# A pre-norm transformer block on one core: one ordinary group of gate and up products fewer, vector work placed by the list, two x tiles on another queue

## The chip, the core and the metric

The kernel runs on one core of a Trainium2 chip. The metric is the device time of one execution in microseconds (us). Engines are named as in the profile: PE multiplies matrices (PEld is its weight load), DVE is the vector engine, ACT the scalar engine, POOL is GpSimd, SP the engine that issues most DMAs.

## The reference, cut to what matters

The input is one sequence of 2048 tokens with 448 features, all in float32. H is 16, the window W is 256, the hidden width of the feed-forward is 1792.

```python
def _A_ref(x, wqkv, wo):                       # sliding-window attention
    ...
    scores = jnp.einsum("bhqd,bhkd->bhqk", q, k) * (Dh ** -0.5)
    mask = (idx[:, None] - idx[None, :] >= 0) & (idx[:, None] - idx[None, :] < W)
    p = _softmax(jnp.where(mask[None, None], scores, -1e9), axis=-1)
    ...
def _B_ref(x, w_gate, w_up, w_down):           # gated feed-forward
    g = jnp.einsum("bsd,df->bsf", x, w_gate)
    u = jnp.einsum("bsd,df->bsf", x, w_up)
    return jnp.einsum("bsf,fd->bsd", _gelu(g) * u, w_down)

h = x + _A_ref(_layernorm(x), A_wqkv, A_wo)
h2 = h + _B_ref(_layernorm(h), B_w_gate, B_w_up, B_w_down)
```

## The kernel before, in words

Every float32 operand of a product is split into a high and a low part (`to_hi` on ACT, line 396; `to_lo` on DVE or POOL, line 399), and a product is three matmuls: high by high, high by low, low by high.

**Order.** The program is not written in the order in which it runs. Each step is handed to a list (`op`, `dma`) with an engine, a key, an expected duration and the tiles that it reads and writes. `Lists.run` then walks through the list in its own model of time, takes at each point the candidate that can start first, the smaller key ahead, and so fixes what stands in which row of each engine. On the chip every engine works through its rows in that order and waits where an operand is late. The constants at the head of the file (keys, lags, engine names) only move rows.

**Attention.** Sixteen blocks (four chunks of 512 tokens by four groups of heads) go through projections (line 678), scores (729), maxima (733, DVE), probabilities (802, with exponentials at 806, ACT), products with v (840) and the output product (900, into `hres`). The first x tiles are loaded into `hres` by `load` in `start` (line 525), all by SP's queue.

**Feed-forward.** The 2048 tokens by 1792 columns fall into fourteen groups of 256 columns by 1024 tokens. Each group needs gate, up, and the product with `w_down`. A gate or up product of a group can be made in two ways:

- *Ordinary* (`cslot`, line 1139, and `cfull`, line 1151): four turns (two halves of the tokens, gate and up), each of 7 slots. A slot is 6 matmuls of 512 columns, two at a time on the two halves of the rows of PE's array. A group is 28 slots.
- *By seven products* in place of eight, after Strassen's scheme (`both`, line 1340): 25 slots of the same 6 matmuls for gate and up together. This asks for sums and differences of pieces of x (`tokens_x`, lines 1051, 1054 and 1057) and of the weights (`weight_set` with `sum_`, line 1210, on POOL), and for sums of the results (`copied`, 1346, ACT; `added`, 1350, DVE).

The first `CL` groups are ordinary; some of their slots fill waits late in the attention. The rest are made by seven products. Between the slots of a later group stand the down products of an earlier one (`down_half`, line 1414). Their halves write the same four banks one after the other, and before the second half may write, ACT reads one element of the bank (`seen`, line 1260). `out_add` (1431) adds the finished rows to `hres`.

**Buffers.** Weights of a group by seven products lie in one of three areas, `wbuf`: the tile `w2` (shown as `w`) and two halves of `proj`. Pieces of x for the first 1024 tokens lie in `xo` (`xarea`, `XPLACE`), which is opened after the attention, and for the last 1024 tokens in `xT`.

## Time and profile before

| | |
|---|---|
| runs | 696.53, 698.39, 698.69 us; median 698.39 us |
| profiled execution | 698.2 us, of which the span from the first to the last instruction is 696.5 us |
| granted clock | 0.999 |
| PE, DVE, ACT, POOL busy | 98%, 74%, 59%, 45% of the span |
| instructions of PE (matmuls) | 5544, of them 450 ordinary gate/up, 1650 by seven products, 1320 down |
| share of the 16 DMA engines | 58% (SP's queue) |

Busy time says how much of a stretch an engine had work in flight. Windows cut the span into stretches, waits say which engine ended another's idle time, the chain follows the end of the program back to what released each step, and the timeline lists instructions in order of time.

### The profile page before, as it was taken

What the parts mean: (1) busy time and instruction counts of PE and PEld (TensorE: products, weight loads), DVE (VectorE), ACT (ScalarE), POOL (GpSimd) and SP (SyncE); (2) the same over time, 40 slices, a digit from 0 to 9 for tenths busy, and PEclk for the clock granted to TensorE, in tenths of its full rate; (3) what the DMA queues carried; (4) which work ended last, traced back from release to release, by engine and by line L of the source; (5) the groups of instructions that cost most, each with busy time, mean ns of one, the idle gap of its engine ahead of it and who ended that gap; (6) DMA issues with size and microseconds to landing.
All of it is one profiled execution on the core that took longest, in us unless ns stands there. A gap on an engine that the chain in (4) does not pass through costs nothing. (4 is left out here: it accounts for less than half of the span.)

```text
span 696.5 us, 15373 instructions
## 1 busy us (share of the span) xinstructions
PE 685.1 (98%) x5544; PEld 578.1 (83%) x5544; DVE 513.4 (74%) x1213; ACT 413.9 (59%) x911; POOL 311.1 (45%) x422
## 2 busy tenths in 40 slices
PE   8999999999999999999999999999999999999997
PEld 7888888888888878878878888888888888888886
DVE  7967678987798788838775789776555756866764
ACT  7747576877768667776554565644534545546431
POOL 5612654644456446441452779634303445447000
PEclk9999999999999999999999999999999999999999
DMA  9997967688688697406767775415004744533102
GB/s 315 277 285 216 286 173 202 183 230 244 166 210 247 183 273 207 165 1 178 197 181 158 213 205 170 119 51 171 20 16 131 211 132 132 161 116 88 44 15 105
DMA packets 104691, 116.25 MB, mean 167 GB/s; under 512 B 44632, under 2 KB 82392, under 8 KB 104040
## 3 DMA queue, kind: packets, MB, share of 16 engines
q1 hardware_dynamic: 104472, 115.17, 58.0%
q8 instruction: 43, 0.70, 0.4%
q14 instruction: 32, 0.26, 0.1%
q10 hardware_dynamic: 144, 0.11, 0.0%
HBM read 84.97 MB, written 44.47 MB: 186 GB/s over the span
## 5 line engine op out<-in xcount | busy, mean ns | idle before, releaser
L733 DVE CUSTOM_DVE_ANT_0 mt<-bank,mt 128x384 bf16<-128x384 f32 (+2 forms) x256 | 126.4, 526 | 26.8 <-PE bank L729 24.8
L806 ACT ACTIVATE pp<-bank 128x384 f32<-128x384 f32 (+1 forms) x188 | 90.8, 527 | 18.5 <-PE bank L802 16.3
L678 PE MATMUL bank<-xT 128*128 128x512 f32 x308 | 96.1, 399 | 0.0
L1340 PE MATMUL bank<-xT,proj 64*128 64x512 f32 x735 | 94.7, 389 | 0.2 <-DVE v L1350 0.2
L1340 PEld LDWEIGHTS bank<-xT,proj 64*128 64x128 f32 x735 | 72.1, 184 | 13.4 <-DVE v L1350 0.8
L729 PE MATMUL bank<-rk,rq 84*128 84x384 f32 (+2 forms) x256 | 81.0, 337 | 0.0
L802 PE MATMUL bank<-rq,rk 104*128 104x384 f32 (+2 forms) x352 | 80.6, 302 | 0.0
L821 POOL TENSOR_SCALAR_AFFINE_SELECT pp<-pp 128x512 f32<-128x512 f32 x96 | 60.6, 651 | 40.2 <-ACT pp L806 38.6
L1414 PE MATMUL bank<-proj,gh 64*128 64x448 f32 x624 | 71.5, 362 | 1.2 <-ACT e L1260 1.2
L802 PEld LDWEIGHTS bank<-rq,rk 104*128 104x128 f32 x352 | 59.4, 190 | 9.3 <-ACT pp L806 1.5
L1431 DVE TENSOR_TENSOR hres<-bank,hres 128x448 f32<-128x448 f32 (+1 forms) x113 | 62.8, 611 | 5.6 <-PE bank L1414 5.6
L1414 PEld LDWEIGHTS bank<-proj,gh 64*128 64x128 f32 x624 | 59.2, 184 | 8.0 <-ACT e L1260 1.9
L678 PEld LDWEIGHTS bank<-xT 128*128 128x128 f32 x308 | 55.6, 189 | 6.8 <-DVE proj L399 0.5
L1210 POOL TENSOR_TENSOR xn<-proj 64x128 f32<-64x128 f32 (+2 forms) x36 | 33.3, 928 | 52.5 <-DMA proj<-gu 46.8
L1260 ACT ACTIVATE e<-bank 1x1 f32<-1x1 f32 x139 | 21.7, 156 | 55.9 <-PE bank L1414 41.3
L729 PEld LDWEIGHTS bank<-rk,rq 84*128 84x128 f32 x256 | 47.6, 189 | 7.0 <-DVE mx L733 1.4
L396 ACT ACTIVATE rq<-bank 8x512 fp32r<-8x512 f32 x64 | 37.7, 589 | 22.1 <-PE bank L760 21.0
L399 DVE TENSOR_TENSOR proj<-proj 128x448 fp32r<-128x448 f32 (+2 forms) x42 | 25.8, 630 | 32.0 <-ACT proj L396 27.0
L624 PE MATMUL bank<-proj,xT 128*128 128x448 f32 (+1 forms) x220 | 49.1, 334 | 0.0
L1340 PE MATMUL bank<-xo,proj 64*128 64x512 f32 x366 | 47.7, 389 | 0.1
L1340 PEld LDWEIGHTS bank<-xo,proj 64*128 64x128 f32 x366 | 36.0, 184 | 7.1 <-DVE v L1350 0.8
L1350 DVE TENSOR_TENSOR raw<-bank,raw 128x512 f32<-128x512 f32 x22 | 15.2, 691 | 35.1 <-PE bank L1340 35.0
(193 smaller groups left out, 1474.3 us busy)
## 6 DMA issues: line engine op xcount, KB each, us to landing
rk<-k SPq DMA_DIRECT2D x44, 336.0 KB
rq<-q SPq DMA_DIRECT2D x32, 336.0 KB
gu<-in_gu_dram SPq DMA_DIRECT2D x18, 480.0 KB
proj<-gu SPq DMA_DIRECT2D x24, 288.0 KB
q<-proj SPq DMA_DIRECT2D x12, 448.0 KB
proj<-down SPq DMA_DIRECT2D x22, 224.0 KB
proj<-gu SPq DMA_DIRECT2D x24, 192.0 KB
k<-proj SPq DMA_DIRECT2D x9, 448.0 KB
```

The costliest lines, as they stand in the source:

```text
L396: nc.scalar.activation(dst, src, AF.Copy)
L624: op("pe", mm(224 * n), 0.29 if n == 1 else 0.38, key + a / 16, lambda a=a, h=h, wb=wb, xb=xb: nc.tensor.matmul(bank[b.k][:, 0:224 * n], x ...
L678: op("pe", mm(512) + 0.002, 0.403, key, lambda a=a, h=h, wb=wb, xb=xb: nc.tensor.matmul(bank[b.k], wqk[m][:, h, wb, :], xT[:, xb, cc * 128 ...
L729: nc.tensor.matmul(bank[b.k][:, o:384], rq[u][0:3 * DH, j, i * 128:i * 128 + 128], rk[u][0:3 * DH, j, m0 * 128:(i + 3) * 128], start=True, ...
L733: nc.vector.tensor_tensor_reduce(junk[s % 2][:, o:384], bank[b.k][:, o:384], mask[:, o:384], 1.0, -BIG, OP.add, OP.max, mx[:, i, j:j + 1])
L802: nc.tensor.matmul(bank[b.k][:, n * i:n * i + n], rk[u][0:104, j + i, m * 128:m * 128 + 128], rq[u][0:104, j + i, lo * 128:(hi + 1) * 128] ...
L806: nc.scalar.activation(pp_cols(o, n)[:, j:j + G], bank[b.k][:, 0:G * n].rearrange("p (g t) -> p g t", g=G), AF.Exp, scale=SCALE)
L821: nc.gpsimd.affine_select(a, a, pattern=[[0, 4], [-cm, 128]], compare_op=op_, fill=0.0, base=0, channel_multiplier=cm)
L1210: arith("pool", w, key + 1, lambda e: e.tensor_tensor(xn_m[HALF[side], o:o + w], a(), b(), op=what), rd, [tok])
L1340: nc.tensor.matmul(bank[b.k], w, xarea(u.cp, xl, xs, side)[:, xk], start=p in (1, 2, 5) and not k and not t, stop=t == 2, tile_position=(6 ...
L1414: nc.tensor.matmul(bank[banks[q].k][:, 0:D], h[oh][0]()[HALF[x], q * 128:q * 128 + 128], d[wh][0]()[HALF[x]], start=not ph and not y and n ...
L1431: op("dve", 0.07 + w * 0.463 / D, 0.163 + w * 0.463 / D, key, lambda: nc.vector.tensor_tensor(hres[:, t, c0:c0 + w], bank[b.k][:, c0:c0 + ...
```

## The change

One group less is ordinary (`CL` 3 becomes 2), so that twelve groups instead of eleven are made by seven products. The list may now choose the engine, POOL or DVE, of the sums for x and for the weights and of their low parts, and the engine, ACT or DVE, of the copies of results (`alts`, switched on by `FLEX`). Pieces of x for the first tokens are placed partly in `xT`, so that some of their loads can go before the attention ends. Two of the first four x tiles are issued by ACT's queue. A finer token (`XTB`) lets the list place matmuls of the high part of x ahead of the low part. Some forty numbers of the list are others; two of their lines stand here.

```diff
-MERGE = (1, 1, 1, 0, 1, 1, 1, 1, 0, 1, 1, 1)
+MERGE = (1, 1, 1, 0, 1, 1, 1, 1, 1, 0, 0, 1)
...
-CL = 3
+FLEX = 'xwc'
+CL = 2
...
+            o.fn = lambda: alts[o.eng][2]()
...
-                cand[o.eng].append(o)
+                for e in o.alts or (o.eng,):
+                    cand[e].append(o)
...
+                if o.alts and min(start_of(x, o)[0] + o.alts[x][1] for x in o.alts) < t + o.alts[e][1]:
+                    continue
...
+    def XTB(t, xb):
+
+        return span("xT", t, 1) if xb == 3 else span("xT", t + (xb > 3) / 2, 0.5)
...
-        for t in range(4):
+        op("pool", 0.1, 0.1, -101, lambda: nc.gpsimd.memset(nhalf, -0.5), (), ["nhalf"])
+        for t in range(2):
             load(t, -100 + t)
+        op("act", 1.35, 1.45, -110, lambda: nc.scalar.activation(rcp[0][0:1, 0:1], nhalf[0:1, 0:1], AF.Copy), ["nhalf"], [("rcp", 0)])
+        for t in range(2, 4):
+            op("act", 0.44, 2.3 + 0.3 * (t - 2), -110 + t, lambda t=t: nc.scalar.dma_start(hres[:, t, :], xr[t * 128:(t + 1) * 128, :]),
+               (), [HR(t)])
...
+    wbuf = wbuf if CL > 2 else [wbuf[2], *wbuf[:2]]
...
-    def arith(eng, n, key, fn, r, w, port=True):
-        cost = 0.1 + n * 0.00225 if eng == "pool" else 0.07 + n * 0.00104
-        op(eng, cost, cost + (0.05 if eng == "pool" else 0.1), key, lambda: fn(nc.gpsimd if eng == "pool" else nc.vector),
-           r, w, port=port)
+    def arith(eng, n, key, fn, r, w, port=True, free_choice=False):
+        ways = {"pool": (0.1 + n * 0.00225, 0.15 + n * 0.00225, lambda: fn(nc.gpsimd), port),
+                "dve": (0.07 + n * 0.00104, 0.17 + n * 0.00104, lambda: fn(nc.vector), port)}
+        cost, lat, go, _ = ways[eng]
+        op(eng, cost, lat, key, go, r, w, port=port, alts=ways if free_choice else None)
...
-            arith("pool", w, key + 1, lambda e: e.tensor_tensor(xn_m[HALF[side], o:o + w], a(), b(), op=what), rd, [tok])
+            arith("pool", w, key + 1, lambda e: e.tensor_tensor(xn_m[HALF[side], o:o + w], a(), b(), op=what), rd, [tok], free_choice="w" in FLEX)
```

In the built programs PE's matmuls go from 5194 to 5168: 168 fewer of `cslot`, 150 more of `both`, 8 fewer of the transposes of `ident` that only fill time at the start. DVE's instructions go from 1215 to 1346, POOL's from 427 to 328, ACT's stay at 914.

**ACT at the start.** Before, ACT's rows begin with the load of its function table and a fill of `rk` (line 569), and the normalised x tiles (449) follow:

```order
L569 ACT_TABLE_LOAD
L569 ACTIVATE rk_186<-e_75 32x1536
L396 ACTIVATE one<-ident 128x128
L449 ACTIVATE xn<-hres,bnve 128x448 x2
L396 ACTIVATE proj<-pp 128x2x224
```

Now the first row is a DMA of an x tile, and a second one stands behind the table load (lines are numbered as in the changed kernel: 550 issues the tiles, 548 brings the table, 467 normalises):

```order
L550 DMA hres<-in_x_dram 128x448
L548 ACT_TABLE_LOAD
L548 ACTIVATE rcp_81<-bnve 1x1
L550 DMA hres<-in_x_dram 128x448
L414 ACTIVATE one<-ident 128x128
L591 ACTIVATE rk_184<-e_75 32x1536
L467 ACTIVATE xn<-hres,bnve 128x448
```

Two DMA issues have moved from SP to ACT, one of them behind the table load; SP's weight loads stand two issues earlier.

**The first weights by seven products.** Before, the sums of the first weight set (in `w`, line 1210) stand on POOL, with sums for x (1057) between:

```order
L1210 TENSOR_TENSOR xn<-w_3359 128x384
L1057 TENSOR_TENSOR e_3360<-xo,raw 64x512
L399 TENSOR_TENSOR xo<-raw,xo 128x512
L1210 TENSOR_TENSOR xn<-w_3359,xn 128x384
L1210 TENSOR_TENSOR xn<-w_3359 64x128
L1210 TENSOR_TENSOR xn<-w_3359,xn 64x384
L1210 TENSOR_TENSOR xn<-w_3359 64x384
L399 TENSOR_TENSOR w_3359<-xn,w_3359 128x384
L1210 TENSOR_TENSOR xn<-proj 64x128
```

Now the first set lies in `proj`, and its sums (line 1237) stand on DVE, behind the products of gate and up (1206) of an ordinary turn and between the low parts (417) and the sums (1081) of x:

```order
L1206 TENSOR_TENSOR v<-bank_174,v 128x512
L1206 TENSOR_TENSOR v<-bank_175,v 128x512
L417 TENSOR_TENSOR xT<-raw,xo 128x512
L1237 TENSOR_TENSOR xn<-proj 128x384
L1237 TENSOR_TENSOR xn<-proj 64x128
L1237 TENSOR_TENSOR xn<-proj,xn 128x384
L417 TENSOR_TENSOR proj<-proj 128x256
L1237 TENSOR_TENSOR xn<-proj,xn 64x384
L1237 TENSOR_TENSOR xn<-proj 64x384
L417 TENSOR_TENSOR proj<-proj 128x384
L1081 TENSOR_TENSOR raw<-raw,xT 64x512
L417 TENSOR_TENSOR proj<-xn,proj 128x128
```

All five sums of this set have moved to DVE's rows.

More of the change, by code (lines that the diff above doesn't have):

```diff
@@ L1009, in load @@
         def load(l, slot, side, c, row, k0=0, n=1):
-            dma(key, 131 * n, lambda: nc.sync.dma_start(f(xarea(cp, l, slot, side)[:, k0:k0 + n]), rows(c, row + 64 * k0, n)),
+            soon = not cp and type(XPLACE[cp][l, slot]) is tuple
+            dma(X0LOAD + 10 * k0 if soon else key, 131 * n, lambda: nc.sync.dma_start(
+                f(xarea(cp, l, slot, side)[:, k0:k0 + n]), rows(c, row + 64 * k0, n)),
                 come(c) + xgate(cp, l, slot), [t for k in range(k0, k0 + n) for t in xtok(cp, l, slot, k, side)], cost=0.61 + 0.03 * n,
-                after=chain[-1:])
+                after=[got[X0HOLD]] if soon else chain[-1:])
         def fill(k, i, c, row):
```

153 lines of the change are left out of this document (83 added, 70 removed).

## The prediction

> **What bounds the kernel now.** I read the page first, then the span cut into stretches, then the timeline of PE where it waits.
>
> ```profile
> PE 685.1 (98%) x5544; PEld 578.1 (83%) x5544; DVE 513.4 (74%) x1213; ACT 413.9 (59%) x911; POOL 311.1 (45%) x422
> ```
>
> PE is in work for 685.1 of 696.5 us, so the time is PE's stream and its few waits. The stretches are: to the first projection, the attention to its last output product, the ordinary groups, the groups by seven products, the tail. Columns: length, then each engine's busy time and its instructions, granted clock, DMA.
>
> ```profile
> core 0: us, PE busy (x) PEld busy (x) DVE busy (x) ACT busy (x) POOL busy (x), PEclk, DMA share, GB/s
> 0.00:14.07 14.07, 10.63 (x75) 9.87 (x76) 9.66 (x21) 10.20 (x17) 9.61 (x29) 1.00 0.88 299
> 14.07:322.57 308.50, 308.40 (x2168) 253.97 (x2166) 243.88 (x774) 217.82 (x430) 143.21 (x241) 1.00 0.74 209
> 322.57:376.45 53.88, 51.94 (x465) 43.06 (x466) 40.49 (x73) 30.03 (x77) 19.31 (x21) 1.00 0.75 189
> 376.45:673.99 297.54, 296.85 (x2696) 256.35 (x2696) 206.86 (x325) 152.39 (x377) 138.94 (x131) 1.00 0.41 119
> 673.99:696.50 22.51, 17.26 (x147) 14.86 (x145) 12.53 (x23) 3.50 (x13) 0.00 (x0) 0.96 0.23 82
> ```
>
> The attention and the eleven groups by seven products have PE busy but for 0.1 and 0.7 us; the clock is full. One group by seven products takes 297.54 / 11 = 27.05 us. The stretch that waits is the third, 1.94 us. Its timeline on PE (start, length, instructions, in brackets the idle time and who ended it):
>
> ```profile
> 336.99 1.37 PE L1414 MATMUL bank<-proj,gh 64*128 64x448 f32 x12
> 338.85 1.50 PE L1414 MATMUL bank<-proj,gh 64*128 64x448 f32 x12 [0.48 <-ACT e L1260]
> 340.19 2.25 PE L1139 MATMUL bank<-xT,proj 64*128 64x512 f32 x18
> ...
> 345.00 2.61 PE L1414 MATMUL bank<-proj,gh 64*128 64x448 f32 x24
> 347.44 4.95 PE L1139 MATMUL bank<-xT,proj 64*128 64x512 f32 x42
> 352.23 1.37 PE L1414 MATMUL bank<-proj,xT 64*128 64x448 f32 x12
> 354.37 1.50 PE L1414 MATMUL bank<-proj,xT 64*128 64x448 f32 x12 [0.77 <-ACT e L1260]
> 355.71 4.97 PE L1139 MATMUL bank<-xT,proj 64*128 64x512 f32 x42
> 360.51 2.61 PE L1414 MATMUL bank<-proj,e 64*128 64x448 f32 x24
> 362.96 4.95 PE L1139 MATMUL bank<-xT,proj 64*128 64x512 f32 x42
> 367.75 1.37 PE L1414 MATMUL bank<-proj,gh 64*128 64x448 f32 x12
> 369.81 1.48 PE L1414 MATMUL bank<-proj,gh 64*128 64x448 f32 x12 [0.69 <-ACT e L1260]
> 371.13 2.88 PE L1139 MATMUL bank<-xT,proj 64*128 64x512 f32 x24
> 373.85 2.60 PE L1414 MATMUL bank<-proj,gh 64*128 64x448 f32 x24
> 376.28 0.63 PE L1340 MATMUL bank<-xo,w 64*128 64x512 f32 x4
> ```
>
> Two readings. Seven ordinary slots (42 matmuls) go from 347.44 to 352.23, so a slot is 4.80 / 7 = 0.686 us. And 24 down matmuls in one piece take 2.44 us where nothing is late (345.00 to 347.44), but 3.20, 3.48 and 3.38 us (from 336.99, 352.23 and 367.75) where ACT's one-element read of the bank came late: 2.74 us lost in three of six pieces.
>
> **Term 1, the products.** A group leaves the ordinary way, 28 slots, for the other, 25. In the chain of waits a slot by seven products costs the same:
>
> ```profile
> 617.00 2.74 PE bank L1340 x24
> 619.74 1.21 PE bank L1414 x12
> 620.95 2.06 PE bank L1340 x18
> ```
>
> Three slots are 18 matmuls, 2.06 us. All of it lies on PE, which is the path: **-2.06 us**. The built program has these 18 matmuls less, so nothing of this term hangs on a choice of the list.
>
> **Term 2, the pieces of down.** Behind the last output product the new order has 27 ordinary slots instead of 53, and two unbroken pieces of 24 down matmuls instead of six; in all other places halves of down stand between products, where ACT's read has time. At the rate of before, one of two pieces late by 2.74 / 3 = 0.91 us, 0.91 stays of 2.74: **-1.83 us**. Bounds: -2.74 with none late, -0.9 with both.
>
> **Term 3, the cover of the first group by seven products.** Its first product stood 53.88 us behind the attention's last output product, and stands now at 27 x 0.686 + 2 x 2.44 = 23.4 us. Call that output product's end T. The first weight set overwrites what this product reads, so it can only be loaded from T on, and its sums are now DVE's, in a row behind the two products of gate and up of an ordinary turn that PE finishes 16 slots behind T, at T + 11.0. DVE then has 21 instructions to the last low part of these weights: 11 of 512 elements, 7 of 384, three short. Their prices without and with POOL at work beside:
>
> ```profile
> 323.50 1.28 DVE L399 TENSOR_TENSOR gh<-raw,gh 128x512 fp32r<-128x512 f32 x2
> 367.14 0.72 DVE L399 TENSOR_TENSOR w<-xn,w 128x384 fp32r<-128x384 f32 x2
> L1368 DVE TENSOR_TENSOR v<-bank,v 128x512 f32<-128x512 f32 x11 | 7.5, 680 | 0.0
> L1368 DVE TENSOR_TENSOR v<-e,v 128x512 f32<-128x512 f32 x11 | 11.1, 1006 | 0.0
> L399 DVE TENSOR_TENSOR proj<-xn,proj 128x384 fp32r<-128x384 f32 x12 | 7.5, 623 | 0.8 <-ACT proj L396 0.8
> ```
>
> Two of 512 in 1.28 us are 0.64 each or less; 1006 ns is the group that meets POOL's sums most. For 384 elements about 0.47 us (of the 0.72 us for one long and one short), and 623 ns as the mean of its group. With the short ones at 0.3: 11 x 0.64 + 7 x 0.47 + 0.9 = 11.2, ready at T + 22.2 and 1.2 us early; with the dear rows 11 x 1.006 + 7 x 0.623 + 0.9 = 16.3, ready at T + 27.3 and 3.9 us late. Behind these weights stand the last third of the x pieces, which PE wants some 1.4 us after the first slot, so that there is no room. POOL has in these rows only three sums and two chains of small ones, so I stay near the cheap end and take **+0.7 us**; bounds 0 and +5.5 (3.9 with four x instructions more at 0.4 dearer). It cannot gain, because PE did not wait there before.
>
> **Term 4, the start.** Columns of the timeline as above.
>
> ```profile
> 0.79 1.28 ACT L569 ACT_TABLE_LOAD   x1 [0.79 <-PEq L1778]
> 0.79 1.81 SPq L525 DMA_DIRECT2D hres<-in_x_dram  x4
> 3.40 0.63 DVE L428 BATCH_NORM_STATS2 bnst<-hres 128x6 f32<-128x448 f32 x1 [1.42 <-DMA hres<-in_x_dram]
> 5.51 0.63 DVE L428 BATCH_NORM_STATS2 bnst<-hres 128x6 f32<-128x448 f32 x1 [0.54 <-DMA hres<-in_x_dram]
> 7.33 0.23 POOL L419 TENSOR_SCALAR bnve<-bnmv 128x2 f32<-128x2 f32 x1 [0.36 <-DVE bnmv L430]
> 14.07 4.30 PE L678 MATMUL bank<-xT 128*128 128x512 f32 x18
> ```
>
> The third tile goes out at once and DVE's wait of 0.54 us for it can go, but POOL works on the third and fourth as a pair and waited 0.36 us only: no more than that is to be had. The fourth tile's issue moves from 2.1 us (the fourth of four in 1.81) behind the first issue (0.45) and the table load (1.28), to 2.6 us, so as much can be lost; ACT's fill of `rk` behind them has until 5.65 us, when ACT first waits for nothing else. I take **0**, bounds -0.4 and +0.5. [...]
>
> **Term 5, the attention.** The same matmuls in another order, and one block more whose products with v are made in two parts (`MERGE`), which brings one change more of PE's array mode. Its price is the pause of PE's weight load at line 840, 15.4 / 72 = 0.21 us:
>
> ```profile
> PEld bank L840 <- issue: 15.4, 72, 0.4
> PEld bank L1340 <- DVE v L1350: 2.7, 6, 0.8
> ```
>
> **+0.2 us**, bounds 0 and +2 for waits that a new order may open; there are 0.1 us to gain by the stretch's idle time.
>
> **Term 6, the groups by seven products.** DVE's additions kept the weight load waiting six times, 2.7 us (row above). With DVE fuller and POOL emptier this may go either way: 0, bounds -2.7 and upward as in the rival below.
>
> **Sum** on the profiled execution's 698.2 us (its span 696.5 and 1.7 around it): 698.2 - 2.06 - 1.83 + 0.7 + 0.2 = **695.2 us**. The profiled execution lies 0.2 us below the median of the runs, 698.39, so I take the sum as the forecast of the median. 0.3% or 2.1 us is about what can be told from no change here; the forecast is 3.2 us below.
>
> **Rivals.**
> *The cover is gone (0.17).* DVE's chain of term 3 is dear: half way to the bound, 3.5 us late instead of 0.7, gives 698.0 us, no change. For it: the 1006 ns row, and that 53.88 us of cover become 23.4. Against: POOL's few instructions there.
> *DVE becomes the bound (0.15), slower.* In the fourth stretch DVE has 206.86 / 11 = 18.8 us of work in each group's 27.05. The 131 instructions that the list gives it besides are 10.9 in each of twelve groups, if all lie there. The point is (27.05 - 18.8) / 10.9 = 0.76 us apiece: at 0.623 a group has 25.6 us and PE still leads; at 0.85, between the 384 and the 1006 ns row, 28.1 us, so 1.0 us a group and 12.4 in all: 707.6 us. Against it: what dear rows there are come from POOL's work, and POOL has 99 instructions fewer.
> *The port set free (0.08), faster still.* If DVE's dear rows become cheap ones as POOL's sums go, the 2.7 us of waits for its additions go with them: 692.5 us. [...]
> That the change does not do what it says is ruled out for the products, which are counted in the built program.
>
> **Numbers.** The forecast has 0.60, of which I put 0.05 above 696.3 us. Faster by over 0.3%: 0.55 + 0.08 = 0.63. Within: 0.17 + 0.05 = 0.22. Slower: 0.15. The range goes down to 692.0 (the port set free, with a little of the start) and up to 699.5, over the dear chain of term 3 (698.0) and most of its bound (695.2 - 0.7 + 5.5 = 700.0); the DVE-bound case is left out above.
>
> **What would show it.** Right: 282 ordinary matmuls and 1800 by seven products; 27.0 us a group as before; at most one pause of PE with ACT's read at its end before the first product of line 1369, which starts some 23.5 us behind the last output product; at that first group a wait for DVE below 1 us; DVE at 80 to 85% of the fourth stretch. Wrong: a wait of several us for DVE's `proj` or `xT` at the first group (first rival); groups of 28 us with PE waiting for DVE throughout (second); a first projection later than 14.6 us; an attention longer than 308.5 - 1.4 us (two ordinary slots fewer stand in it) by more than 1 us.

## The result and the profile after

The changed kernel takes 709.52 us (median of five runs, 708.89 to 711.16), the kernel before 698.39 us beside it (696.53 to 699.25): a ratio of 1.0173, 95% interval 1.0151 to 1.0196. The forecast of 695.2 us and its range (692.0 to 699.5) missed; the sign was that of the rival to which 0.15 was given. The profiled execution took 709.5 us, its span 707.8. The page's first part, and the span cut at the points of the prediction (first projection, last output product, first product by seven, last one):

```profile
PE 689.3 (97%) x5518; PEld 602.1 (85%) x5518; DVE 561.0 (79%) x1344; ACT 413.8 (58%) x909; POOL 200.7 (28%) x323
0.00:15.61 15.61, 11.03 (x56) 9.99 (x56) 9.17 (x21) 10.39 (x17) 11.04 (x28) 0.78 0.91 319
15.61:324.82 309.21, 308.74 (x2170) 254.44 (x2168) 243.69 (x776) 215.73 (x427) 142.92 (x243) 1.00 0.77 209
324.82:353.10 28.28, 25.19 (x211) 20.74 (x212) 25.95 (x46) 16.98 (x40) 4.67 (x4) 0.94 0.62 142
353.10:684.93 331.83, 327.16 (x2944) 302.22 (x2942) 269.71 (x481) 167.24 (x414) 42.10 (x49) 1.00 0.46 126
684.93:707.80 22.87, 17.23 (x147) 14.76 (x145) 12.53 (x23) 3.50 (x13) 0.00 (x0) 0.93 0.23 81
```

Work has gone from POOL (311.1 to 200.7 us) to DVE (513.4 to 561.0 us), and DVE is now in work for 25.95 of the 28.28 us ahead of the first product. The granted clock is no longer full in two stretches, 8.28 to 15.11 and 346.20 to 349.61 us (0.50 in both). Against the prediction's own sum (T is the end of the last output product):

| | forecast | measured | more |
|---|---|---|---|
| start and attention, to T | 322.57 - 1.37 + 0.2 = 321.4 | 324.8 | 3.4 |
| T to the first product by seven | 23.4 + 0.9 + 0.7 = 25.0 | 28.3 | 3.3 |
| twelve groups | 12 x 27.05 = 324.6 | 331.8 | 7.2 |
| tail | 22.5 | 22.9 | 0.4 |

The groups, of 150 products each, take 29.59, 27.24, 27.23, 30.19, 29.23, 26.87, 26.87, 27.10, 27.01, 27.04, 27.63 and 25.84 us: the excess is in the first, the fourth and the fifth; the eleventh has 0.6 us of it. PE's waits, with who ended them, in us, times, longest:

```profile
PE bank L1445 <- ACT e L1288: 3.1, 1, 3.1
PE bank L472 <- ACT xn L467: 2.4, 2, 1.9
PE bank L1751 <- POOL ident L573: 2.1, 1, 2.1
PE bank L1369 <- DVE xo L417: 1.9, 1, 1.9
PE bank L1369 <- DVE v L1381: 1.3, 2, 1.1
```

The first is one pause in front of the second half of the first down product. PE's timeline shows it and what comes behind it:

```profile
340.53 1.37 PE L1445 MATMUL bank<-proj,gh 64*128 64x448 f32 x12
344.99 1.61 PE L1445 MATMUL bank<-proj,gh 64*128 64x448 f32 x12 [3.09 <-ACT e L1288]
346.40 4.42 PE L1166 MATMUL bank<-xT,w 64*128 64x512 f32 x24
350.65 2.61 PE L1445 MATMUL bank<-proj,gh 64*128 64x448 f32 x24
353.10 0.39 PE L1369 MATMUL bank<-xo,proj 64*128 64x512 f32 x2
```

24 ordinary matmuls take 4.42 us; the 24 ahead of the pause took 2.88. ACT's rows tell why its read (L1288) came late, and some of DVE's rows why ACT was:

```profile
340.59 0.53 ACT L414 ACTIVATE proj<-proj 128x384 fp32r<-128x384 f32 x1 [0.84 <-DMA xn<-v]
341.02 0.75 ACT L467 ACTIVATE raw<-hres,bnve 128x448 f32<-128x448 f32 x1
341.68 0.29 ACT L414 ACTIVATE proj<-xn 128x128 fp32r<-128x128 f32 x1
342.89 0.52 ACT L414 ACTIVATE proj<-xn 128x384 fp32r<-128x384 f32 x1 [0.93 <-DVE xn L1237]
343.32 1.06 ACT L1191 ACTIVATE v<-bank 128x512 f32<-128x512 f32 x2
344.28 0.63 ACT L414 ACTIVATE xo<-raw 128x512 fp32r<-128x512 f32 x1
344.80 0.34 ACT L1288 ACTIVATE e<-bank 1x1 f32<-1x1 f32 x2
...
336.87 1.43 DVE L417 TENSOR_TENSOR xo<-e,xo 128x512 fp32r<-128x512 f32 x1 [1.33 <-ACT xo L414]
338.21 1.28 DVE L1206 TENSOR_TENSOR v<-bank,v 128x512 f32<-128x512 f32 x2
...
340.01 0.86 DVE L1237 TENSOR_TENSOR xn<-proj 128x384 f32<-128x384 f32 x2
...
348.86 0.54 DVE L417 TENSOR_TENSOR proj<-xn,proj 128x384 fp32r<-128x384 f32 x1
```

The read stands behind high parts of the first weights, which wait for transfers (0.84 us ahead of the pause) and for DVE's sums (0.93 us in it); the rest of the pause is ACT's own work in the rows ahead of the read. In the fourth and fifth group it is DVE itself; windows of groups 4 and 5, and DVE's rows where PE waits 1.86 us for the last of them but one:

```profile
437.20:467.30 30.10, 28.50 (x249) 24.05 (x247) 28.85 (x46) 17.90 (x42) 8.78 (x6) 1.00 0.52 146
467.30:496.60 29.30, 27.44 (x251) 26.18 (x249) 23.50 (x40) 12.60 (x32) 3.15 (x4) 1.00 0.36 97
464.94 1.77 DVE L1084 TENSOR_TENSOR v<-xT,v 64x512 f32<-64x512 f32 x1
466.64 1.49 DVE L417 TENSOR_TENSOR e<-v,e 128x512 fp32r<-128x512 f32 x1
468.06 1.48 DVE L417 TENSOR_TENSOR xo<-xo,xT 128x512 fp32r<-128x512 f32 x1
469.47 0.67 DVE L1381 TENSOR_TENSOR raw<-bank,raw 128x512 f32<-128x512 f32 x1
...
463.36 2.81 POOL L417 TENSOR_TENSOR xo<-v,xT 128x512 fp32r<-128x512 f32 x1 [0.42 <-ACT e L1288]
466.25 1.34 POOL L1237 TENSOR_TENSOR xn<-proj 64x384 f32<-64x384 f32 x1
467.67 1.33 POOL L417 TENSOR_TENSOR proj<-proj 128x384 fp32r<-128x384 f32 x1
```

DVE has 28.85 us of work in 30.10, and instructions that take 0.67 us at 344.78 and 346.58 us, with POOL idle, take 1.5 to 1.8 here beside POOL's. Four such rows in group 4 take 3.9 us more than 0.67 each, as much as the group's excess. No run sets DVE free of POOL there and leaves it the same rows, so how much of the loss is the number of rows and how much their price stays open.

### The profile page after: what moved, and what is told of

It is laid out like the page before. It is cut to its first block, busy times and chain, and to the rows that moved or that the text cites. A ratio compares the mean times of both kernels' runs of the same rounds, so it can differ in the third digit from the quotient of the medians.

```text
span 707.8 us, 15249 instructions
## 1 busy us (share of the span) xinstructions
PE 689.3 (97%) x5518; PEld 602.1 (85%) x5518; DVE 561.0 (79%) x1344; ACT 413.8 (58%) x909; POOL 200.7 (28%) x323
## 4 chain that ended last, share of the span: by engine, by line
PE 84%; DVE 10%; DMA 2%; issue 2%; ACT 1%; POOL 0%; SPq 0%; DVEq 0%; ACTq 0%
PE bank L1369 25%; PE bank L1445 16%; PE bank L700 10%; PE bank L824 7%; PE bank L751 6%; PE bank L862 6%; PE bank L646 5%; PE bank L922 4%; PE bank L1178 2%; DVE hres L1462 2%; PE bank L1166 1%; PE bank L472 1%; DVE xo L417 1%; DMA xo<-xn 1%; DVE xT L417 1%
## 5 line engine op out<-in xcount | busy, mean ns | idle before, releaser
L755 DVE CUSTOM_DVE_ANT_0 mt<-bank,mt 128x384 bf16<-128x384 f32 (+2 forms) x256 | 126.8, 525 | 27.8 <-PE bank L751 26.0
L1369 PE MATMUL bank<-xT,proj 64*128 64x512 f32 x627 | 121.6, 388 | 0.0
L1369 PE MATMUL bank<-xo,proj 64*128 64x512 f32 x552 | 111.9, 390 | 3.1 <-DVE xo L417 1.9
L1445 PE MATMUL bank<-proj,gh 64*128 64x448 f32 x672 | 82.2, 365 | 3.8 <-ACT e L1288 3.1
L1369 PEld LDWEIGHTS bank<-xT,proj 64*128 64x128 f32 x627 | 81.2, 184 | 4.4
L1369 PEld LDWEIGHTS bank<-xo,proj 64*128 64x128 f32 x552 | 72.3, 184 | 8.2 <-DVE xo L417 2.3
L1445 PEld LDWEIGHTS bank<-proj,gh 64*128 64x128 f32 x672 | 69.7, 184 | 9.4 <-ACT e L1288 3.5
L1369 PE MATMUL bank<-xT,w 64*128 64x512 f32 x330 | 63.8, 390 | 0.0
L1288 ACT ACTIVATE e<-bank 1x1 f32<-1x1 f32 x132 | 20.7, 157 | 66.9 <-PE bank L1445 51.8
L1369 PE MATMUL bank<-xo,w 64*128 64x512 f32 x255 | 54.0, 389 | 0.4 <-DVE raw L1381 0.4
L646 PE MATMUL bank<-proj,xT 128*128 128x448 f32 (+1 forms) x220 | 51.9, 341 | 0.0
L1369 PEld LDWEIGHTS bank<-xT,w 64*128 64x128 f32 x330 | 43.0, 184 | 3.1 <-DVE v L1381 0.6
```

Of the source, the lines that this page charges most:

```text
L646: op("pe", mm(224 * n), 0.29 if n == 1 else 0.38, key + a / 16, lambda a=a, h=h, wb=wb, xb=xb: nc.tensor.matmul(bank[b.k][:, 0:224 * n], x ...
L755: nc.vector.tensor_tensor_reduce(junk[s % 2][:, o:384], bank[b.k][:, o:384], mask[:, o:384], 1.0, -BIG, OP.add, OP.max, mx[:, i, j:j + 1])
L1369: nc.tensor.matmul(bank[b.k], w, xarea(u.cp, xl, xs, side)[:, xk], start=p in (1, 2, 5) and not k and not t, stop=t == 2, tile_position=(6 ...
L1445: nc.tensor.matmul(bank[banks[q].k][:, 0:D], h[oh][0]()[HALF[x], q * 128:q * 128 + 128], d[wh][0]()[HALF[x]], start=not ph and not y and n ...
```

## The experiments

All runs in one table. First projection, T, the time from T to the end of the first group by seven products, and groups 4 and 5 together are read off each profile; the ratio is to the kernel before on the same chip. Medians less than some 2 us apart are not told apart: the intervals of e1, e2, e3, e5, e7, e14 and e17 overlap the changed kernel's, those of e6, e10 and e12 just reach it. The profile of e16 is of the slowest of its runs (698.54 to 703.88 us), that of e14 too.

| kernel | median us | ratio, 95% interval | first proj. | T | T to end of group 1 | groups 4+5 |
|---|---|---|---|---|---|---|
| changed | 709.52 | 1.0151 to 1.0196 | 15.61 | 324.82 | 57.87 | 59.42 |
| e1 four by SP | 710.15 | 1.0163 to 1.0225 | 18.03 | 327.13 | 55.92 | 59.41 |
| e2 filled pause | 708.40 | 1.0137 to 1.0182 | 13.89 | 324.01 | 55.81 | 59.46 |
| e3 weight sums POOL | 711.20 | 1.0159 to 1.0232 | 14.18 | 323.72 | 58.14 | 61.10 |
| e5 start of before | 708.29 | 1.0122 to 1.0170 | 14.78 | 323.49 | 57.99 | 59.38 |
| e6 halves apart | 707.43 | 1.0113 to 1.0156 | 13.64 | 324.21 | 58.29 | 57.12 |
| e7 second x earlier | 709.17 | 1.0141 to 1.0191 | 14.08 | 324.15 | 58.04 | 59.70 |
| e8 no weight sums | 698.61 | 0.9997 to 1.0020 | 15.61 | 324.78 | 52.75 | 56.62 |
| e9 second x as before | 706.69 | 1.0111 to 1.0141 | 13.90 | 323.71 | 58.60 | 56.27 |
| e10 its times only | 707.36 | 1.0098 to 1.0159 | 14.84 | 323.82 | 58.57 | 56.49 |
| e12 filled transition | 707.60 | 1.0111 to 1.0156 | 14.46 | 324.11 | 55.74 | 59.45 |
| e14 first weights earlier | 709.62 | 1.0139 to 1.0190 | 13.73 | 324.63 | 60.22 | 56.97 |
| e15 cures together | 703.96 | 1.0056 to 1.0106 | 13.32 | 324.10 | 56.39 | 56.30 |
| e17 weights fixed | 711.67 | 1.0186 to 1.0221 | 13.75 | 324.55 | 62.35 | 54.77 |
| e18 no choice | 719.94 | 1.0304 to 1.0337 | 14.03 | 323.75 | 65.01 | 55.42 |
| *three ordinary groups:* before | 698.39 | | 14.07 | 322.64 | 80.57 | |
| e4 three ordinary | 704.62 | 1.0090 to 1.0122 | 13.54 | 324.23 | 82.53 | |
| e11 before, halves apart | 700.85 | 1.0026 to 1.0061 | 14.17 | 322.62 | 82.79 | |
| e13 free choice on before | 705.75 | 1.0087 to 1.0130 | 14.75 | 322.87 | 82.60 | |
| e16 x and copies free | 701.47 | 1.0039 to 1.0080 | 14.68 | 322.87 | 83.86 | |

**Which engine does the sums.** Theory: DVE's row is what groups 1, 4 and 5 wait for; rivals: transfers, or POOL. First the sums moved to POOL in the given order (e3; `emit` names the engine, whatever the list chose):

```diff
-what), rd, [tok], free_choice="w" in FLEX)
+what), rd, [tok], free_choice="w" in FLEX, emit=nc.gpsimd)
```

> The changed kernel with all sums of weight pieces issued on POOL, at the places of the order that the list gave them; 82 instructions leave DVE. Theory (DVE's row is what the groups 1, 4 and 5 and the turn to the first group by seven products wait for): DVE has 3 us less in a group, groups 1, 4 and 5 together lose 3 to 6 of their 7 us of excess, the pause of 3.09 us with ACT's read shrinks, time 703 to 706. Rival (late pieces of x and weights by DMA set these waits): groups 4 and 5 stay at 59 us together, time 709 to 710. Second rival (POOL's sums cost DVE what they save, by the dear rows of 1.0 us beside POOL): groups stay long, DVE's additions go from 0.68 to 0.8 us or more, time 708 to 712.

No gain: POOL takes 1.0 us for a sum where DVE takes 0.55, T to the first product grew from 28.3 to 30.0 us, and groups 4 and 5 from 59.42 to 61.10. The second rival had the time right; the additions `v<-e,v` went from 683 to 751 ns, short of its 0.8 us. So the same sums left out, in an unchanged order, so that products work on other data (e8):

```diff
-arith("pool", w, key + 1, lambda e: e.tensor_tensor(xn_m[HALF[side], o:o + w], a(), b(), op=what), rd, [tok], ...
+arith("pool", w, key + 1, lambda e: None, rd, [tok], ...
```

> The changed kernel without the sums and differences of weight pieces: all 100 are left out, 82 of them on DVE, so that DVE has 45 us of work less and POOL 15 us less; everything else, the low and high parts of what stands in their place too, is done. Theory (DVE's row in groups 1, 4 and 5 and ahead of the first product is full, and fills because of these sums): groups 1, 4 and 5 lose 4 us or more of their 7.1 us of excess, the first product comes 24.5 to 26.5 us behind the output product's end in place of 28.3; time 699 to 703. Rival (the x pieces of the last tokens and the exclusion of DVE and POOL set groups 4 and 5; the weights do not): groups 4 and 5 stay above 58 us together, time 705 to 709.

698.6 us, 10.9 less than the changed kernel, with the windows from T to the first product, of the first group, and of groups 6 to 12:

```profile
324.78:349.96 25.18, 23.82 (x211) 19.57 (x212) 23.47 (x42) 16.75 (x41) 1.28 (x1) 1.00 0.71 170
349.96:377.53 27.57, 27.50 (x249) 23.70 (x247) 21.75 (x43) 15.79 (x40) 5.98 (x11) 1.00 0.71 176
488.45:675.55 187.10, 187.10 (x1716) 187.10 (x1714) 121.34 (x220) 88.98 (x224) 4.86 (x6) 1.00 0.35 104
```

Without these sums the first product stands 25.18 us behind T, the pause with ACT's read falls from 3.09 to 1.10 us, group 1 takes 27.57, groups 4 and 5 lose 2.8 of 5.3 us of excess. Of the 10 us less of span 5.1 lie between T and the end of group 1. The clock is full in these windows, which is part of it (below). The run takes away DVE's work and also the wait of the high and low parts for the sums; it does not separate the two. Is then the free choice the loss? It alone, with `alts` in the list and in the calls that the change gives it, was added to the kernel before (e13):

```diff
+FLEX = 'xwc'
...
```

> The kernel before, with its three ordinary groups, its tables, its start and its placing of x, and only the free choice of the engine for the sums of x and of weights, their low parts and the copies (FLEX xwc) added. Theory (the free choice fills DVE's row, but with 54 us of cover ahead of the first product there is room; what it costs comes at the second x pieces): within 2 us of before, 697 to 700. Rival (the free choice itself is the loss, wherever it stands): 701 us or more. Second rival (it is a gain by itself, groups of 26.9 in place of 27.06 us): 695.5 to 697.

The first rival: 705.75 us, with 54 us of cover. The windows of T to the first product and of the first three groups:

```profile
322.87:378.08 55.21, 52.29 (x462) 42.61 (x464) 43.99 (x79) 29.67 (x76) 12.42 (x15) 1.00 0.72 184
378.08:405.47 27.39, 27.24 (x249) 24.46 (x246) 23.81 (x45) 14.93 (x38) 2.46 (x3) 1.00 0.67 190
405.47:437.40 31.93, 29.42 (x249) 24.01 (x247) 31.65 (x51) 18.06 (x44) 13.29 (x12) 1.00 0.54 151
437.40:465.17 27.77, 27.65 (x248) 25.29 (x246) 22.82 (x42) 14.77 (x35) 2.91 (x3) 1.00 0.40 121
```

In the second group DVE has 31.65 us of work in 31.93: it is the bound there, where the weights' sums, the second x pieces and the additions meet; 4.3 of the 8.0 us of longer span lie in this group, and no other is over 27.8 us. Which part of the choice it is (e16):

```diff
+FLEX = 'xc'
```

> The kernel before with the free choice for the sums and low parts of x and for the copies of results, but not for the weights (FLEX xc): DVE has 19 rows more in place of 135, POOL 10 fewer. Theory (it is the weights' choice that fills DVE's row): time within 1.5 us of before, 697 to 699.5, no group above 28 us. Rival (x or the copies, or any new order of the rows, cost it): 701 us or more.

701.5 us, about half of that loss: the choice for x and copies, with the order that goes with it, costs some 4 us already (a pause of 2.75 us with ACT's read, groups of 29.3 and 28.6 us), the one for weights the rest. What two groups are worth without it, first with the weights fixed on POOL (e17, `FLEX = 'xc'` in the changed kernel):

> The changed kernel without the free choice for the weights (FLEX xc): their sums stand on POOL, as before, and the list orders its rows by that; DVE has 118 rows less. Theory (two ordinary groups leave POOL too little time for the first weights, 1.0 us a sum, so that the choice only moved the loss): the first product comes 33 to 38 us behind the output product in place of 28.3, the groups behind it are 27 to 27.5 us with DVE at 80% or less of them, time 704 to 710. Rival (DVE's row was all, POOL has the time): first product 30 us or less, time 699 to 703.

PE's timeline:

```profile
348.04 1.48 PE L1445 MATMUL bank<-proj,gh 64*128 64x448 f32 x12 [0.93 <-ACT e L1288]
357.24 1.69 PE L1369 MATMUL bank<-xo,proj 64*128 64x512 f32 x4 [7.27 <-DVE proj L417]
```

The first product began at 24.8 us, where the theory had 33 to 38, but stopped at once for 7.27 us for its weights: POOL's sums of them run from 337.4 to 346.3 us. And with no choice at all (e18; `WLO2`, `XADD2`, `XLO`, `XLO2`, `XTIME` and `XLATE` are as before):

```diff
-FLEX = 'xwc'
+FLEX = ''
...
```

> The changed kernel with no free choice at all (FLEX empty) and with the engine names of before for the sums and low parts of x and of weights, and the second x pieces at the times of before: two ordinary groups, the start of the changed kernel, its tables elsewhere. Theory (with the cover of 28 us the engines of before are too slow for x and weights of the first group): first product 35 to 40 us behind the output product, time 708 to 716. Rival (two groups are a gain once the choice is off): below 700 us.

719.9 us, longer than even the theory had it, and not where it had it: the first product comes at 28.8 us, and the groups behind it take 36.2, 27.1, 32.1 and 28.5 us. So two groups with the tables and the start of the change and the engines of before are some 22 us behind the kernel before, and the free choice gives 10 of them back; with three groups and the tables of before the choice costs 8.

**The cover.** The other direction, three groups in the changed kernel (e4; here part of the feed-forward works on other data than the reference's, in the same number and sizes of instructions):

```diff
-CL = 2
+CL = 3
```

> The changed kernel with three ordinary groups in place of two, everything else as changed. Theory (the change of the number of groups itself loses what it saves because its cover of 54 us shrinks to 28; starts and engine choices cost the rest): the start and the attention stay as slow as in the changed kernel (first projection 15.6 us, 2.5 to 3.5 us lost against before), the first product by seven comes without a wait over 1 us, the half clock at 346 us is gone, the two groups with the second x pieces stay 4 to 5 us too long; time 704 to 708. Rival (the number of groups is a pure gain and the choices of engines are all the loss): slower than the changed kernel by the 2.06 us of the products, 710 to 712. Second rival (engine choices are harmless with three groups, the cover was all): 700 to 702.

704.6 us: in the theory's range, and 4.9 us less than with two groups. The first projection did not stay late (13.54 us, see the start below). The first product comes 54.8 us behind T; the two groups with the second x pieces are still 29.9 and 29.0 us.

**The transition.** The first half of the first down product three times over, to fill the pause (e12; `again` is 3 for that half and 1 for the others):

```diff
-lambda j=j: go(j, h, d),
+lambda j=j: [go(j, h, d) for _ in range(again)],
```

> The changed kernel with the first half of the first down product issued three times over (24 matmuls of 2.4 us more on PE, the same values each time), so that they fill the pause of 3.09 us. Theory (the pause costs once as idle time and again by the half clock behind it): the pause falls to 0.5 to 0.9 us, the granted clock stays at 1.0 around 346 us, the next 24 ordinary matmuls take 2.9 us in place of 4.42, the first product comes 1.2 to 1.8 us earlier, time 1 to 2 us shorter, 707.5 to 708.5. Rival (DVE's row is the bound behind it, and the faster matmuls only wait there): first product or end of the first group within 0.5 us of the changed kernel's 57.9 us behind the output product.

```profile
339.82 3.81 PE L1447 MATMUL bank<-proj,gh 64*128 64x448 f32 x36
344.01 1.50 PE L1447 MATMUL bank<-proj,gh 64*128 64x448 f32 x12 [0.38 <-ACT e L1288]
345.34 2.93 PE L1166 MATMUL bank<-xT,w 64*128 64x512 f32 x24
```

The theory holds: same wait for ACT, but PE kept in work, the 24 matmuls take 2.93 us, and T to the end of the group is 2.1 us shorter. The price of the half clock shows without any filler too: e1 and e2 (below) have the rows of the changed kernel here and pauses of 3.03 and 2.87 us, no half clock came behind them, and the stretch took 55.9 and 55.8 us, where the changed kernel, with half a clock behind its pause, took 57.87. Then the halves set apart (e6):

```diff
                 cslot(key + 2 * j, 2 * m + ty, c, 1, j, banks)
+                if m and j == 1:
+                    pause(ckey(x) + 11)
...
-                pause(ckey(x) + 20)
```

> The changed kernel with the two halves of a down product between the ordinary slots set apart: the first half of each pair stands behind the second slot of the turn in place of behind the fourth, so that ACT's read has two slots, 1.4 us, of cover. The list orders the other rows by itself. Theory (the pause of 3.09 us is ACT's read in a row behind work that waits for weights and DVE; DVE's row to the first group by seven products is as late): the pause with ACT's read is gone or below 1 us, but a wait for DVE of 1 to 3 us stands at the first group by seven products in its place; end of the output product to first product 26 to 28 us; time 706.5 to 709. Rival (only the place of the read costs, DVE is on time): first product 24 us behind the output product's end, time 704.5 to 706.

The pause with ACT is 0.41 us, the first product starts 24.95 us behind T, and 3.48 us for DVE stand at the first group instead (`[3.48 <-DVE xT L417]`, half a clock behind it: 12 down matmuls take 2.38 us, 1.50 ahead of it); T to the end of the group is 58.29 us, nothing won there; the 2 us less of time are in groups 4 and 5. The first weights earlier (e14, `WFIRST` 1380 to 1100):

> The changed kernel with the key of the first weights by seven products at 1100 in place of 1380, so that their transfers go some 3 to 5 us earlier, ahead of x pieces. Theory (DVE's row between the output product and the first group is full whatever comes first): the wait moves to a piece of x or to an addition, output product to end of the first group stays at 56 to 58.5 us, time within 1.5 us of 709.5. Rival (the weights' transfer is the late part): that stretch falls to 52 to 54.5 us, time 705 to 706.

The wait moved again, to DVE (2.61 us for `xT`, 2.1 for L1206). The time stayed, as the theory had it, but the stretch grew to 60.22 us, above the theory's range, and groups 4 and 5 fell to 56.97: earlier weights are no cure, though the order in the full row is not without effect.

**The second x pieces.** First the key alone (e7, `XLATE` 250 to 150):

> The changed kernel with one number of the list other: the key of the x pieces for the last 1024 tokens (XLATE) is 150 as before in place of 250, so that their sums and low parts stand earlier in the rows. Theory (groups 4 and 5 wait because DVE and POOL reach these pieces in a row that is full and shut each other out): groups 4 and 5 fall from 59.4 to 55 to 57.5 us together, the wait of 1.9 us for a piece in xo goes, time 2 to 4 us shorter. Rival (the transfers of these pieces are late and no order of sums helps): groups 4 and 5 stay at 58.5 us or more, PE's wait ends with the same line.

The rival: 59.70 us, nothing won. Then times and engines of before (e9), and the times alone (e10, the first four lines):

```diff
-XTIME = (9, 7, 8)
+XTIME = (10, 6, 6)
-XLATE = 250
+XLATE = 150
-XADD2 = ('dve', 'dve', 'pool', 'pool')
+XADD2 = ('pool', 'pool', 'dve', 'dve')
-XLO2 = ('dve', 'dve', 'dve', 'pool', 'dve')
+XLO2 = ('pool', 'pool', 'dve', 'pool', 'dve')
-free_choice="x" in FLEX)
+free_choice="x" in FLEX and not cp)
```

> The changed kernel with the x pieces of the last 1024 tokens made as before: their parts enter the list at the steps of before (XTIME 10, 6, 6), with the key of before (XLATE 150), and their sums and low parts have the fixed engines of before (three sums by pool, pool, dve, low parts by pool, pool, dve, pool, dve). Weights and the pieces of the first tokens keep the free choice. Theory (groups 4 and 5 are late because these pieces were put on DVE's row, and late in it): the groups around 437 to 497 us fall from 59.4 to 54.5 to 56.5 us together, and no other group rises by over 0.7 us; time 3 to 5 us shorter, 704.5 to 706.5. Rival (DVE's weight sums fill the row there whoever makes the x pieces, and what is won in one group is lost in the next): the five first groups stay within 1.5 us of 143.5 us together; time 708 to 710.

> As the kernel with the second x pieces as before, but only their times and key (XTIME 10, 6, 6 and XLATE 150); engines stay free. Theory (the time at which the pieces are loaded and made counts, the engine does not): the same gain as with the fixed engines within 1 us. Rival (the engine counts: the free choice puts them on DVE where POOL would do): less than half of that gain, groups 4 and 5 at 57.5 us or more together.

Groups 4 and 5 fall to 56.27 and 56.49 us: it is the step at which the pieces are taken up (`XTIME`, with `XLATE`), not the engine. The times, 706.7 and 707.4 us, are just above the theory's range.

**The start.** Tiles 2 and 3 by SP at their place in the order (e1):

```diff
-lambda t=t: nc.scalar.dma_start(hres[:, t, :], xr...
+lambda t=t: nc.sync.dma_start(hres[:, t, :], xr...
```

> The changed kernel with one word other: x tiles 2 and 3 are issued by SP's queue at the same place of the order, so that ACT's queue has no x tile. Theory (the third tile, in flight beside the first, delays the first tile by 1.0 us, the pause of 1.87 us follows from that, and the half clock from the pause): DVE's first statistics start below 3.6 us in place of 4.44, the pause of PE before the first transpose is below 1 us, no half clock before 15 us, first projection at 14.0 to 14.6 us in place of 15.61, time 1.5 to 2.5 us shorter, 707 to 708. Rival (the order of the rows at the start, the other keys and the finer tokens of the high and low parts, makes the projections late, not the queue): first projection stays at 15.3 us or later, time 709 to 710.

Neither: the third tile's issue now stood first in SP's queue (first statistics at 3.93 us), the fourth stood behind weights (its statistics started at 9.19 us), the first projection came at 18.03, and PE ran at half clock up to there (the 11 matmuls of line 646 ahead of it take 2.66 us, 1.47 in e2; last section). All four tiles by SP ahead of the weights, ACT's two issues left out (e5):

```diff
-        for t in range(2):
-            load(t, -100 + t)
+        load(0, -100)
+        dma(-99, 224, lambda: [nc.sync.dma_start(hres[:, t, :], xr...) for t in (1, 2, 3)], (), [HR(1)])
```

> The changed kernel with the four x tiles issued by SP's queue one after the other ahead of the weights, as before; every other engine has the rows of the changed kernel. Theory (two tiles of two queues in flight together delay the first one): DVE's first statistics start at 3.4 to 3.6 us in place of 4.44, PE's pause before the first transposes is below 1 us, first projection at 13.3 to 14.3 us, time 1 to 2 us shorter than the changed kernel. Rival (the start is lost to rows and to the half clock, which a pause brings or not by where it falls, not to the first tile): the first statistics come early, but the first projection is no earlier than 15 us, or the output product's end stays at 324 us or later; time within 0.7 us of 709.5.

The first statistics on DVE, in the changed kernel and in this one:

```profile
4.44 0.63 DVE L446 BATCH_NORM_STATS2 bnst<-hres 128x6 f32<-128x448 f32 x1 [2.46 <-DMA hres<-in_x_dram]
3.33 0.63 DVE L446 BATCH_NORM_STATS2 bnst<-hres 128x6 f32<-128x448 f32 x1 [1.35 <-DMA hres<-in_x_dram]
```

The first tile comes 1.1 us earlier; the first projection, 14.78, missed the theory's 14.3, since a pause of 1.48 us for the next tile again had half a clock behind it (four transposes at 11.04 us take 1.11 us, those at 8.74 took 0.66). T is 1.3 us earlier and the time 1.2 us shorter, but see the end of this section. Filler in the first pause (e2):

```diff
         def tr():
+            for _ in range(16 if kind == "ln1" and t == 0 else 0):
+                nc.tensor.transpose(bank[b.k][:, 0:128], ident, ident)
```

> The changed kernel with 16 more transposes of ident on PE just ahead of the first transposes of x, as filler in the pause of 1.87 us; x tiles as in the changed kernel. Theory (a pause of about two us is what brings the half clock of 8.28 to 15.11 us): the pause falls below 0.5 us, the granted clock stays at 1.0 through the first 20 us, and the first projection comes 0.5 to 1.5 us earlier, at 14.1 to 15.1 us; time 0.5 to 1.5 us shorter. Rival (the late tile alone costs the time, PE waits for x anyway): the clock stays up but the first projection stays at 15.4 to 15.7 us, time within 0.3 us of 709.5. Second rival (the clock goes by something else): half clock at 8.3 us as before.

The filler removes the pauses, no slow stretch follows, and the first projection comes at 13.89, but T only 0.8 us earlier: PE then waits for DVE's low parts (0.81 us at 17 us). The time is 1.1 us shorter. Neither this gain nor that of e5 is told from chance: e3, e4, e6 to e10, e12, e14, e17 and e18 have the changed kernel's rows on every engine for the first 280 us, and their profiles have first projections from 13.54 to 15.61 us and T from 323.71 to 324.78. Of e2 and e5 only the T of e5, 323.49, lies outside, by 0.2 us.

**Together, and before improved.** The edits of e5, e2, e12 and e9 in one kernel (e15):

> The changed kernel with four edits together: four x tiles by SP's queue ahead of the weights, 16 filler transposes in the first pause, the first half of the first down product three times over, and the second x pieces made as before. Theory (these losses are apart and add up: 1.2, 0.5 to 1, 1 to 2 and 2.8 us): 702.5 to 704.5 us, still 4 to 6 us behind the kernel before. Rival (they share one cause and do not add up): 705.5 us or more.

704.0 us: in the theory's range, though the four medians, 1.2, 1.1, 1.9 and 2.8 us, sum to 7.0 and the gain is 5.6. The kernel is still 5.6 us behind the kernel before. The edit of e6 on the kernel before (e11):

> The kernel before with the two halves of a down product between the ordinary slots set apart, the first one behind the second slot of the turn. Theory (in the kernel before the 2.74 us of the three pieces with a late read are a loss of PE, which has 20 us of cover there and nothing else late): the pauses with ACT's read are gone, the time is 1.0 to 2.5 us shorter, 695.5 to 697. Rival (DVE's row is as late there, as in the changed kernel: the wait comes back at the first group by seven products): a wait of 1 us or more for DVE at the first product, time within 1 us of before, or longer by the array's changes.

Slower, 700.85 us: the pauses are gone, and 1.05 us for DVE and 1.14 us for ACT stand in the first two groups (29.55 and 29.09 us). No version tried beat the kernel before.

## Why the prediction was wrong

**Term 1** held: 18 matmuls fewer, paid as priced. **Term 2** had the count right, one late read in two pieces, and its size wrong: 0.91 us was the mean of the pieces of before, with pauses of 0.48 to 0.77 us; this pause was 3.09 us, in an ACT row that waited for transfers and for DVE's sums, and the half clock behind it took 4.42 - 2.93 = 1.5 us more. These two are nearly all of the 3.3 us more from T to the first product. **Term 3** is the step that failed first: it took DVE's chain as something that only the first product waits for. The chain itself was priced well: from L1206 at 338.21 to the last low part at 349.40 are 11.2 us, the cheap estimate. It began at T + 13.4 and not T + 11.0, behind a low part that waited 1.33 us for an x piece, and ended at T + 24.6, still ahead of the first product at T + 28.3, which did not wait for it. But ACT's row, the read in it and DVE's later rows stand behind the same chain, so that T to the end of group 1 was 57.9 us where 25.0 + 27.05 = 52.1 were forecast; e8, without the weights' sums, has 52.75. e6 and e14 show that mending one wait brings out the next. That the shrinking cover was the risk was seen; that two groups with the old engines end some 22 us behind (e18) was not.

**Term 4** had its bounds wrong. It took the third and fourth tile as what could be late; with two queues in flight the first one is (4.44 against 3.33 us). The fourth was not held up by the table load: ACT's queue issued it at 1.29 us. The first projection came at 15.61 us, and with 12 matmuls of line 646 fewer ahead of it (18 in place of 30, 0.11 us each at full clock), so that the start is 1.54 + 1.3 = 2.9 us late. It is the latest of twelve profiles with these rows; the earliest is at 13.54. **Term 5** took 0.2 us for one pause more of the weight load; at line 862 it now pauses 74 times for 16.0 us, two pauses and 0.6 us more than before. The attention, 309.21 us where 308.50 - 1.37 + 0.2 = 307.3 were forecast, is 1.9 us over: 0.4 by these pauses, and 1.3 by those 12 matmuls, which stand in it now. Start and attention together came out 3.4 us late, 2.3 to 3.4 in the twelve profiles. The half clock of 8.28 to 15.11 us is in it; what else makes the start late stays open, since no run tells the tile order apart from chance.

**Term 6** is the largest miss, 7.2 us. It set 0, and its rival spread DVE's 131 added instructions over twelve groups and found the point at 0.76 us apiece. That mean hid where they fall. In groups 6 to 12 DVE has room, and they are as fast as before or faster, but for the eleventh; in groups 1 and 4 it has 27.2 and 28.9 us of work in 29.6 and 30.1, and the fifth begins with a wait for the fourth's rows. The right rival was there with the wrong place: DVE is late in three groups and in the stretch ahead of them, while its share of the whole stretch, 81%, is what was forecast. The twelve groups take 331.8 us; with the second x pieces at their old steps 329.2 (e9), without the weights' sums 325.6 (e8). The two overlap, and no run has both.

Two more things stay open. The kernels with other choices have another order behind the attention, and e18 keeps the tables of the change, so that the loss of the choice, of its order and of the missing group aren't separated. And the three-group kernels show that the choice costs 4 to 8 us, but not which single rows do.

## What to carry to other kernels

An engine that is 80% busy over a stretch (DVE in e13 from T to the last product by seven, 285.4 of 358.7 us) can be 99% busy in the one group that matters (31.65 of 31.93 us): ask for the load of the helper engines per stage, at the stages where several preparations meet, before work is moved to them. Work that hides preparation has a price, and taking some away is paid in waits elsewhere even where every chain fits by itself. And a pause of PE is paid twice when the clock drops behind it (here 3.09 us, and 1.5 us more in the next 24 matmuls).

## What the runs showed of the hardware

**The clock.** Some of PE's pauses were followed by half a clock and some were not, and not by their length alone. Windows of the changed kernel around its two slow stretches, of e16 around its pause of 2.75 us, of e17, and of e1 behind a pause of 3.03 us:

```profile
8.28:15.11 6.83, 6.27 (x28) 5.70 (x29) 4.52 (x10) 5.25 (x11) 6.41 (x9) 0.50 1.06 383
346.20:349.61 3.41, 3.41 (x20) 2.71 (x18) 3.41 (x7) 1.61 (x3) 0.08 (x1) 0.50 0.15 38
357.56:360.97 3.41, 3.41 (x20) 2.80 (x18) 1.32 (x2) 0.63 (x2) 0.00 (x0) 0.50 0.83 225
352.60:362.84 10.24, 5.60 (x27) 4.78 (x29) 7.95 (x15) 2.76 (x7) 4.71 (x5) 0.50 0.54 122
347.30:350.70 3.40, 3.40 (x32) 2.93 (x34) 3.40 (x7) 2.76 (x6) 0.00 (x0) 1.00 0.16 51
```

The slow stretches last 3.41 us or two or three times that (6.83 and 10.24); 2.75 us of pause brought one, 3.03 us did not. The changes of clock of the changed kernel, at 4.87, 8.28, 15.11, 346.20, 349.61 and 704.60 us, lie on one grid of 3.413 us (0, 1, 3, 100, 101 and 205 steps behind the first), and so do the two of the kernel before, at 5.24 and 694.73 us (202 steps). In the changed kernel PE is idle for 1.88 us of the step from 4.87 to 8.28 and for 2.20 us of that from 342.79 to 346.20, and the step behind each has half a clock; it is idle for 1.34 us of the step from 465.67 to 469.08, and the clock behind it stays full. In e16 all 2.75 us lie in the step ahead of the slow one. For e1 only an estimate can be had: its matmuls come to full pace at the first projection, 18.03 us, and 96 steps of 3.413 us from there an edge, at 345.7 us, would split its pause (344.21 to 347.24 us) into some 1.5 and 1.5 us. So the idle time within one step tells these cases apart: 1.88, 2.20 and 2.75 us had half a clock behind them, 1.34 and, by the estimate, 1.5 us had not.

At the start the granted clock has a gap: the trace has no entry ahead of its first full-clock one (4.87 us in the changed kernel, 5.24 before), and the windows count the gap as full. The changed kernel's transposes in it stand 0.213 us apart, as in the slow stretch that follows, and 0.109 at full clock. So PE starts at half clock there, and it does for a length that differs from run to run: the first 18 transposes take 3.50 us in the changed kernel, 3.67 before, and 4.10 in e1, e2, e4 and e5. Those of the changed kernel and of e2:

```profile
2.14 3.50 PE L1751 MATMUL bank<-ident 128*128 128x128 f32 x18 [2.14 <-POOL ident L573]
2.14 4.10 PE L1753 MATMUL bank<-ident 128*128 128x128 f32 x18 [2.14 <-POOL ident L575]
```

**DVE beside POOL.** The same addition, one group in each kernel: 1006 ns before, 683 ns with POOL's work down from 311.1 to 200.7 us. Before, six of its eleven met no POOL instruction and took 676 to 686 ns, the five that met one 945 to 1510; the same addition with `bank` as its first input took 675 to 684 ns, three of eleven beside POOL's.

```profile
L1399 DVE TENSOR_TENSOR v<-e,v 128x512 f32<-128x512 f32 x12 | 8.2, 683 | 0.0
```

This gain of the "port set free" rival is real in this row, 0.32 us an instruction, and the kernel was slower all the same; in group 4 other rows were dear instead (1.5 to 1.8 us, above). There the rows of the two engines end in turn from 466 us on, POOL's at 466.17, 467.59 and 469.00 us, DVE's at 466.71, 468.13 and 469.54, each of DVE's 0.54 us behind POOL's, and POOL's low part of 463.36 us takes 2.81 us, where the two that met no work of DVE took 1.29.
